# Alternating first-layer and second-layer units of a feed-forward block that runs beside attention

## The chip, the cores and the metric

The kernel runs on one core of one Trainium2 chip. The metric is the device time of one execution in microseconds (us). Before the change three runs took 1277.15, 1279.8 and 1281.62 us; the median is 1279.8 us.

## The reference

Thresholded attention is followed by a two-layer feed-forward block with no routing:

```python
scores = scale * q @ k.T                       # 8 batches, 8 heads, 576 tokens, head size 64
thresh = max(scores, -1) - tau                 # tau = 0.02
scores = where(scores >= thresh, scores, -1e9)
attn   = softmax(scores)                       # per row of 576
x      = (attn @ v), heads side by side        # 4608 tokens x 512
h      = x @ w_in                              # 512 x 2048
g      = h / (1 + exp(-h))
out    = g @ w_out                             # 2048 x 512
```

All inputs are float32.

## The kernel before, in words

**Attention.** The scores of one batch are worked off in 36 tiles of up to 128 query rows by 576 keys (`tiles`, 288 in all). For tile t, `scores` (L412) makes the scores in PSUM with four matrix products on TensorE. There are two such score buffers of two banks each. `soft1` takes the row maximum on VectorE (L422), `soft1b` the exponential on ScalarE (L432), `soft2` the threshold mask and the row sum on VectorE (L441, the last reader of the score buffer), `soft2b` the scaling on ScalarE (L454), and `soft3` splits the weights into two 16-bit parts on GpSimd (L465, L468, L471) and has them transposed by DMA. `av` (L496) multiplies by the values, and `av_post` (L514, L515) stores the result as the tiles `x16` of that batch. There are two sets of `x16`, for even and odd batches.

**Feed-forward.** Tokens are handled in chunks, two per batch: 288 and 288 columns (256 and 320 in batch 0). A chunk (b, c0, n) has 32 units. Sixteen are first-layer units: `h_unit` f makes 128 rows of h with 12 matrix products (L530) into one PSUM bank. Its `post` then runs four operations on that bank: tanh on ScalarE (L538), a product on VectorE (L539), a 16-bit copy into `gbuf` on ScalarE (L546) and the remainder of that rounding into `gbuf` on VectorE (L547), which releases the bank. The other sixteen are second-layer units: `o_unit` (d, quarter) adds 12 matrix products (L562) to the bank of output rows d. Each quarter uses four of the sixteen g tiles; after the fourth quarter a `post` copies the bank to memory on ScalarE (L572) and a DMA writes it out.

**Banks.** PSUM has four banks for scores, one for `av`, and three named m0, m1 and m2 that `bank` hands out in turn to whatever asks next (in turn over two of them early on, over three from the middle of batch 0). h units, o units and the small product of `pow2_scales` (L118, the maximum of a batch's values over all partitions) share them.

**Order.** `moe_units` yields all 16 h units of a chunk and then all 16 o units. The main loop walks over the tiles; when a chunk's `x16` is ready it appends the chunk's units to the list `units` and sets a rate (units per tile, such that 95% of the list is worked off by the time of the next batch). `step_unit` emits one unit's matrix products and then the `post` of the unit before. After the last tile at least four units are emitted per step. The framework then orders each engine's instructions at compile time, by priority and by a timeline that it simulates; each engine runs its own list strictly in that order. `scores` and `av` have a raised priority.

**gbuf** is one area in SBUF with 17 slots of 2 x 320 16-bit numbers, handed out in turn. Before batch 0's units need it, parts of it serve for loading weights (L158 to L160) and for the zero-padded queries of the first visits (L333).

Of the kernel before, what the change touches and what calls it, by code (L numbers as in the profile page):

```python
# [9 lines left out]
F16 = mybir.dt.float16  # L10
# [9 lines left out]
P = 128  # L20
B, H, S, D = 8, 8, 576, 64
NPAIR = H // 2
DM, DFF = 512, 2048
NK = DM // P
NF = DFF // P
HALF = S // 2
WID = 320
EXPMASK = 0x7F800000
GB = 17
WSPARE = 2  # L30
LOAD = 5
AV_LAG = 3
# [20 lines left out]
def attention_moe(  # L53
# [10 lines left out]
    nc = tc.nc  # L64
    const = ctx.enter_context(tc.tile_pool(name="const", bufs=1))
    sb = ctx.enter_context(tc.tile_pool(name="sb", bufs=2))
    gbuf = const.tile([P, GB * 2 * WID], F16, name="gbuf")
    xp = [ctx.enter_context(tc.tile_pool(name="x0", bufs=1))]
    stage_ctx = ExitStack()
    stage = stage_ctx.enter_context(tc.tile_pool(name="stage", bufs=2))  # L70
# [5 lines left out]
    turn = [0, 2]  # L76

    def bank(shape, name, own=None):
        if own is None:
            own = turn[0] = (turn[0] + 1) % turn[1]  # L80
        return ps_m.tile(shape, F32, tag=f"m{own}", name=name)
# [7 lines left out]
        out=gate, in0=tau_sb, scalar1=0.0, scalar2=0.125, op0=ALU.is_ge, op1=ALU.mult  # L89
# [3 lines left out]
        out=ntau, in0=tau_sb, scalar1=0.0, scalar2=-1.0, op0=ALU.max, op1=ALU.mult  # L93
# [6 lines left out]
    for i in range(2):  # L100
        t = const.tile([P, S + 64], F32R, name=f"qstack{i}")
# [4 lines left out]
    def pow2_scales(mx, name, across=True):  # L106


        k = name[0]
        one = const.tile([P, 1], F32, name=f"{name}_one", tag=f"{k}_one")  # L110
        nc.vector.tensor_reduce(out=one, in_=mx, op=ALU.max, axis=AX.X)
        if across:


            diag = const.tile([P, P], BF16, name=f"{name}_diag", tag="diag")
            nc.scalar.activation(diag, ident, AF.Copy, scale=one)
            allp = bank([P, P], f"{name}_ps")
            nc.tensor.matmul(allp, ones, diag, start=True, stop=True)  # L118
            one = const.tile([P, 1], F32, name=f"{name}_all", tag=f"{k}_all")
            nc.vector.tensor_reduce(out=one, in_=allp, op=ALU.max, axis=AX.X)  # L120
        cl = const.tile([P, 1], F32, name=f"{name}_cl", tag=f"{k}_cl")
        nc.vector.tensor_scalar(
            out=cl, in0=one, scalar1=2.0**-20, scalar2=2.0**47, op0=ALU.max, op1=ALU.min
        )
        e2 = const.tile([P, 2], I32, name=f"{name}_e2", tag=f"{k}_e2")
        nc.vector.tensor_scalar(
            out=e2[:, 0:1], in0=cl.bitcast(I32), scalar1=EXPMASK, scalar2=None, op0=ALU.bitwise_and
        )
        nc.vector.tensor_scalar(
            out=e2[:, 1:2], in0=cl.bitcast(I32), scalar1=EXPMASK, scalar2=EXPMASK,  # L130
            op0=ALU.bitwise_and, op1=ALU.bitwise_xor,
        )
        sc = const.tile([P, 2], F32, name=f"{name}_sc", tag=f"{k}_sc", bufs=3)
        nc.vector.tensor_scalar(
            out=sc[:, 0:1], in0=e2[:, 1:2].bitcast(F32), scalar1=2.0**12, scalar2=None, op0=ALU.mult
        )
        nc.vector.tensor_scalar(
            out=sc[:, 1:2], in0=e2[:, 0:1].bitcast(F32), scalar1=2.0**-13, scalar2=None, op0=ALU.mult
        )
        return sc  # L140
# [75 lines left out]
    def wi(c, f, lo):  # L216
        col = f * P
        o = (512 if lo else 0) + col % 512
        return w16[:, NK * (col // 512) + c, o : o + P]

    def wo(f, d, lo):
        o = (512 if lo else 0) + d * P
        return w16[:, 4 * NK + f, o : o + P]
# [108 lines left out]
    for i in range(2):  # L332
        t = gbuf.bitcast(F32)[:, 4096 + 512 * i : 4608 + 512 * i]  # L333
# [185 lines left out]


    gt = {}
    gcount = [0]
    po = {}

    def h_unit(b, c0, n, f):
        ph = bank([P, 512], f"h_{b}_{c0}_{f}")
        k = 0
        for c in range(NK):
            for lo_w, lo_x in ((0, 0), (0, 1), (1, 0)):
                nc.tensor.matmul(  # L530
                    ph[:, :n], wi(c, f, lo_w), x16[b, lo_x][:, c, c0 : c0 + n],
                    start=(k == 0), stop=(k == 11),
                )
                k += 1

        def post():
            th = sb.tile([P, WID], F32, tag="th", name=f"th_{b}_{c0}_{f}", bufs=2)
            nc.scalar.activation(th[:, :n], ph[:, :n], AF.Tanh, scale=moe_sc[b][:, 0:1])  # L538
            nc.vector.scalar_tensor_tensor(  # L539
                out=ph[:, :n], in0=th[:, :n], scalar=1.0, in1=ph[:, :n],  # L540
                op0=ALU.add, op1=ALU.mult,
            )
            o = 2 * WID * (gcount[0] % GB)
            gcount[0] += 1
            g = gbuf[:, o : o + 2 * WID].rearrange("p (r n) -> p r n", r=2)
            nc.scalar.activation(g[:, 0, :n], ph[:, :n], AF.Copy, scale=2.0**-14)  # L546
            nc.vector.scalar_tensor_tensor(  # L547
                out=g[:, 1, :n], in0=ph[:, :n], scalar=2.0**-14, in1=g[:, 0, :n],
                op0=ALU.mult, op1=ALU.subtract,
            )  # L550
            gt[b, c0, f] = g

        return post

    def o_unit(b, c0, n, d, quarter):
        if quarter == 0:
            po[b, c0, d] = bank([P, 512], f"o_{b}_{c0}_{d}")
        ps = po[b, c0, d]
        for f in range(4 * quarter, 4 * quarter + 4):
            g = gt[b, c0, f]  # L560
            for k, (lo_w, lo_g) in enumerate(((0, 0), (0, 1), (1, 0))):
                nc.tensor.matmul(  # L562
                    ps[:, :n], wo(f, d, lo_w), g[:, lo_g, :n],
                    start=(f == 0 and k == 0), stop=(f == NF - 1 and k == 2),
                )

        def post():
            if quarter < 3:
                return

            o = wst[:, NW + d % 2, :]
            nc.scalar.activation(o[:, :n], ps[:, :n], AF.Copy, scale=moe_sc[b][:, 1:2])  # L572
            c = b * S + c0
            nc.sync.dma_start(out=outT[d * P : (d + 1) * P, c : c + n], in_=o[:, :n])

        return post

    def moe_units(b, c0, n):
        for f in range(NF):
            yield lambda f=f: h_unit(b, c0, n, f)  # L580
        for d in range(DM // P):
            for quarter in range(4):
                yield lambda d=d, quarter=quarter: o_unit(b, c0, n, d, quarter)


    visits = [(0, p, kind) for kind in ("low", "high") for p in range(NPAIR)]
# [6 lines left out]
    ready = []  # L593
    start = {}
    for v, (b, p, kind) in enumerate(visits):
# [19 lines left out]
        if kind == "low":  # L615
            at(u - LOAD, lambda v=v: load_direct(v))
            at(u - 2, lambda v=v: scale_direct(v))
            c0, n = ranges[0]
# [13 lines left out]
    NT = len(tiles)  # L632
# [43 lines left out]
    units = []  # L676
# [4 lines left out]
    def run_posts():  # L681
        for f in post:
            f()
        post.clear()
# [6 lines left out]
    def live(t):  # L691
        return 0 <= t < NT and tiles[t] is not None

    scores(0)
    t = 0
    while t < NT + 8 or units or ready:
        while ready and ready[0][0] <= t:
            _, b, c0, n = ready.pop(0)
            units.extend(moe_units(b, c0, n))
            nxt = [r[0] for r in ready if r[0] > t + 1]  # L700
            rate = len(units) / max(1, (nxt[0] if nxt else NT + 8) - t)
            rate *= RATE
            if b == 0:
                rate = RATES[0 if c0 == 0 else 1]
        if t >= first_high + 20:
            turn[1] = 3
        if live(t):
            pri(PRI_SOFT1, lambda: soft1(t))()
        if live(t + 1):
            pri(PRI_S, lambda: scores(t + 1))()  # L710
        if live(t - 1):
            soft2b(t - 1)
        if live(t):
            pri(PRI_SOFT1, lambda: soft1b(t))()
        if live(t - 1):
            soft3(t - 1)
        for f in todo.pop(t, []):
            f()
        credit += rate
        if t >= NT:  # L720
            credit = max(credit, 4.0)
        if units and credit >= 1:
            step_unit()
            credit -= 1
        if live(t):
            pri(PRI_SOFT2, lambda: soft2(t))()
        for v, p, c0, n in avs.pop(t, []):
            b = visits[v][0]
            if v in direct:
                a_ps = av_direct(v, p)  # L730
            else:
                a_ps = pri(PRI_AV, lambda v=v, p=p, c0=c0, n=n: av(v, p, c0, n))()
            run_posts()
            scale = xscale if v in direct else 2.0**-12
            post.append(lambda b=b, p=p, c0=c0, n=n, a_ps=a_ps, scale=scale: av_post(b, p, c0, n, a_ps, scale))
        while units and credit >= 1:
            step_unit()
            credit -= 1
        if not units:
            credit = 0.0  # L740
            run_posts()
        t += 1
# [42 lines left out]
```

## Time and profile before

| | |
|---|---|
| three runs | 1277.15, 1279.8, 1281.62 us |
| span of the profiled execution (first to last instruction) | 1276.2 us |
| own device time of the profiled execution | not listed apart from its span |
| TensorE busy | 1152.4 us (90%) |
| VectorE busy | 967.7 us (76%) |
| ScalarE busy | 819.6 us (64%) |
| GpSimd busy | 751.1 us (59%) |
| mean granted TensorE clock | 0.969 |

PE stands for TensorE's matrix products, PEld for its weight loads, DVE for VectorE, ACT for ScalarE, POOL for GpSimd, SP for the queue that issues DMAs. "L530" is line 530 of the kernel before. A group's row ends with the idle time of its engine just before those instructions, and with what ended that idle time. Since every engine runs its list in order, an instruction that waits holds up all that stands behind it on its engine.

### The profile page before, as it was taken

The numbers are of one execution on the slowest core, as the hardware profiler recorded it, in microseconds if no ns is written. First come the engines' busy times: TensorE is split into PE (matmuls) and PEld (weight loads), VectorE is DVE, ScalarE is ACT, GpSimd is POOL, SyncE is SP. The second block draws the span as 40 slices with busy tenths as digits, with TensorE's granted clock in tenths as the row PEclk, the third lists the DMA queues.
The fourth block names the chain that finished last, engine by engine and source line by source line (L and its number), as shares of the span: only waits on it lengthen the run. The fifth ranks groups of instructions, "written<-read, shape, count | busy, mean of one in ns | idle before, by whom it ended". The sixth has DMA issues, their size and how long they took to land.

```text
span 1276.2 us, 27018 instructions
## 1 busy us (share of the span) xinstructions
PE 1152.4 (90%) x9400; PEld 898.8 (70%) x9400; DVE 967.7 (76%) x2627; ACT 819.6 (64%) x1505; POOL 751.1 (59%) x952
## 2 busy tenths in 40 slices
PE   5774768898899998998989999998999999999998
PEld 3453657676678776776767777786777777777777
DVE  7899998987988989888688858977598848521431
ACT  5787776765867867777476747866477746532431
POOL 4568977787678777874568608781478508300000
PEclk8886989998999999999989999999999999999999
DMA  9457768688778787873768538781687418300000
GB/s 301 121 183 179 172 119 163 138 151 168 135 151 154 135 168 161 156 146 79 152 122 157 114 85 158 148 156 39 129 159 144 103 24 140 72 15 18 8 15 19
DMA packets 363480, 158.15 MB, mean 124 GB/s; under 512 B 329552, under 2 KB 338256, under 8 KB 363344
## 3 DMA queue, kind: packets, MB, share of 16 engines
q1 hardware_dynamic: 363344, 156.43, 59.0%
q8 instruction: 74, 1.21, 0.4%
q14 instruction: 62, 0.51, 0.1%
HBM read 66.72 MB, written 9.44 MB: 60 GB/s over the span
## 4 chain that ended last, share of the span: by engine, by line
PE 52%; DVE 25%; ACT 6%; DMA 5%; issue 5%; POOL 5%; SPq 1%; POOLq 0%; ACTq 0%; DVEq 0%
PE o L562 22%; PE h L530 15%; PE a L496 7%; PE s L412 7%; DVE w L441 6%; DVE sm L422 5%; DVE qstack L316 4%; DMA wT<-hl 3%; ACT w L432 2%; DVE h L539 2%; DVE gbuf L547 2%; POOL hl L468 1%; DMA vraw<-in_vL 1%; ACT w L454 1%; POOL hl L465 1%
## 5 line engine op out<-in xcount | busy, mean ns | idle before, releaser
L530 PE MATMUL h<-x,wst 128*128 128x288 f16 (+2 forms) x3072 | 416.9, 291 | 23.1 <-DVE gbuf L547 19.4
L562 PE MATMUL o<-gbuf,wst 128*128 128x288 f16 (+2 forms) x3072 | 397.3, 287 | 2.5 <-DVE gbuf L547 1.4
L530 PEld LDWEIGHTS <-wst 128*128 128x128 f16 x3072 | 295.0, 99 | 114.9 <-issue 32.0
L562 PEld LDWEIGHTS <-wst 128*128 128x128 f16 x3072 | 291.9, 98 | 85.5 <-issue 8.3
L468 POOL TENSOR_TENSOR hl<-w,hl 128x512 f16<-128x512 f32 x272 | 328.1, 1206 | 15.9 <-ACT hl L463 2.1
L465 POOL TENSOR_SCALAR hl<-w 128x576 f16<-128x576 f32 x264 | 181.5, 690 | 236.6 <-ACT w L454 133.0
L432 ACT ACTIVATE w<-s,sm 128x576 f32<-128x576 f32 x288 | 211.2, 738 | 106.5 <-DVE sm L422 32.2
L441 DVE SCALAR_TENSOR_TENSOR w<-s,sm,w 128x576 f32<-128x576 f32 x288 | 232.7, 812 | 51.1 <-ACT w L432 49.1
L454 ACT ACTIVATE w<-w,sm 128x576 f32<-128x576 f32 x288 | 219.5, 772 | 68.7 <-DVE sm L449 59.5
L422 DVE TENSOR_REDUCE sm<-s 128x1 f32<-128x576 f32 x288 | 216.0, 751 | 55.4 <-PE s L412 51.8
L412 PE MATMUL s<-khi,qstack 128*128 128x288 f32 x608 | 158.7, 342 | 37.2 <-DVE w L441 29.9
L539 DVE SCALAR_TENSOR_TENSOR h<-th,h 128x288 f32<-128x288 f32 (+2 forms) x256 | 116.6, 456 | 80.9 <-ACT th L538 75.8
L538 ACT ACTIVATE th<-h,msc 128x288 f32<-128x288 f32 (+2 forms) x256 | 127.1, 500 | 30.7 <-PE h L530 27.7
L496 PE MATMUL a<-wT,v 128*64 128x288 f16 (+1 forms) x1680 | 131.8, 297 | 14.4 <-DMA wT<-hl 14.1
L546 ACT ACTIVATE gbuf<-h 128x288 f16<-128x288 f32 (+2 forms) x256 | 104.0, 408 | 63.5 <-DVE h L539 62.9
L547 DVE SCALAR_TENSOR_TENSOR gbuf<-h,gbuf 128x288 f16<-128x288 f32 (+2 forms) x256 | 115.0, 452 | 37.9 <-ACT gbuf L546 36.4
L412 PEld LDWEIGHTS s<-khi,qstack 128*128 128x128 f32 x608 | 96.8, 194 | 64.3 <-issue 39.7
L412 PE MATMUL s<-klo,qstack 128*128 128x288 f32 x608 | 133.1, 300 | 0.0
L326 POOL TENSOR_TENSOR klo<-kraw,khi 128x576 fp32r<-128x576 f32 x64 | 93.0, 1453 | 53.9 <-ACT khi L324 52.4
L496 PEld LDWEIGHTS <-v 128*64 128x64 f16 x1680 | 93.7, 112 | 42.1 <-issue 33.3
L412 PEld LDWEIGHTS s<-klo,qstack 128*128 128x128 f32 x608 | 100.2, 193 | 1.0 <-issue 0.2
L471 POOL TENSOR_TENSOR hl<-w,hl 128x64 f16<-128x64 f32 x272 | 94.0, 345 | 0.0
(84 smaller groups left out, 876.5 us busy)
## 6 DMA issues: line engine op xcount, KB each, us to landing
qraw<-in_qT SPq DMA_DIRECT2D x128, 144.0 KB, 3.0
kraw<-in_kT SPq DMA_DIRECT2D x128, 144.0 KB, 3.0
vraw<-in_vL SPq DMA_DIRECT2D x32, 320.0 KB, 3.8
wraw<-in_w_out SPq DMA_DIRECT2D x16, 512.0 KB, 3.9
out_t<-wst SPq DMA_DIRECT2D x56, 144.0 KB, 2.4
wT<-hl SPq DMA_TRANSPOSE x304, 3.4
gbuf<-in_w_in SPq DMA_DIRECT2D x8, 512.0 KB, 7.9
wraw<-in_w_in SPq DMA_DIRECT2D x8, 512.0 KB, 5.4
```

What stands on the lines that cost most here:

```text
L412: nc.tensor.matmul(s_ps[:, j, :HALF], lhs, kk[:, j * HALF : (j + 1) * HALF], start=(n == 0), stop=(n == len(seq) - 1),)
L422: nc.vector.tensor_reduce(out=negm, in_=s_ps[:, :, :HALF], op=ALU.max, axis=AX.XY, negate=True)
L432: nc.scalar.activation(wtile[t].rearrange("p (j c) -> p j c", j=2), sps[t][:, :, :HALF], AF.Exp, bias=small[t][:, 0:1],)
L441: nc.vector.scalar_tensor_tensor(out=w3, in0=s_ps[:, :, :HALF], scalar=sm[:, 1:2], in1=w3, op0=ALU.is_ge, op1=ALU.mult, accum_out=sm[:, 2:3],)
L454: nc.scalar.activation(w, w, AF.Copy, scale=r)
L465: nc.gpsimd.tensor_scalar(out=fl[:, 0:S], in0=w, scalar1=1.0, scalar2=1.0, op0=ALU.mult, op1=ALU.mult)
L468: nc.gpsimd.tensor_tensor(out=fl[:, 640:1152], in0=w[:, 0:512], in1=fl[:, 0:512], op=ALU.subtract)
L496: nc.tensor.matmul(a_ps[odd * D : (odd + 1) * D, :n], vt[:, lo_v, odd, kv, :], wT[v, b * H + 2 * p + odd][:, kw, c0 - base : c0 - base + n ...
L530: nc.tensor.matmul(ph[:, :n], wi(c, f, lo_w), x16[b, lo_x][:, c, c0 : c0 + n], start=(k == 0), stop=(k == 11),)
L539: nc.vector.scalar_tensor_tensor(out=ph[:, :n], in0=th[:, :n], scalar=1.0, in1=ph[:, :n], op0=ALU.add, op1=ALU.mult,)
L547: nc.vector.scalar_tensor_tensor(out=g[:, 1, :n], in0=ph[:, :n], scalar=2.0**-14, in1=g[:, 0, :n], op0=ALU.mult, op1=ALU.subtract,)
L562: nc.tensor.matmul(ps[:, :n], wo(f, d, lo_w), g[:, lo_g, :n], start=(f == 0 and k == 0), stop=(f == NF - 1 and k == 2),)
```

## The change

From batch 1 on, the h units of a chunk are no longer followed by its own o units. Each h unit of chunk c is followed by one o unit of chunk c-1. The first chunk of batch 1 has h units alone, and the o units of the last chunk come by themselves at the end. Batch 0 keeps its order. So that two chunks' g tiles can live at once, `gbuf` grows from 17 slots of 640 numbers to 18432 numbers per partition (16 x 2 x 576), and a chunk gets a contiguous region of it (`place_g`). The memory for it comes from the area reserved for DMA descriptors, which is set to 1 KB. In the alternating part the banks are fixed: even h units have m0, odd ones m1, and all o units m2; from the middle of batch 0 on the small product of `pow2_scales` has m0. The o units at the very end take banks in turn.

```diff
-GB = 17
+GWORDS = 2 * NF * S
...
-    gbuf = const.tile([P, GB * 2 * WID], F16, name="gbuf")
+    gbuf = const.tile([P, GWORDS], F16, name="gbuf")
...
-            allp = bank([P, P], f"{name}_ps")
+            allp = bank([P, P], f"{name}_ps", 0 if turn[1] == 3 else None)
...
-    def h_unit(b, c0, n, f):
-        ph = bank([P, 512], f"h_{b}_{c0}_{f}")
+    def place_g(b, c0, n):
+        if gnext[0] + 2 * NF * n > GWORDS:
+            gnext[0] = 0
+        gbase[b, c0] = gnext[0]
+        gnext[0] += 2 * NF * n
+
+    def h_unit(b, c0, n, f, own=None):
+        if f == 0:
+            place_g(b, c0, n)
+        ph = bank([P, 512], f"h_{b}_{c0}_{f}", own)
...
-            o = 2 * WID * (gcount[0] % GB)
-            gcount[0] += 1
-            g = gbuf[:, o : o + 2 * WID].rearrange("p (r n) -> p r n", r=2)
+            o = gbase[b, c0] + 2 * n * f
+            g = gbuf[:, o : o + 2 * n].rearrange("p (r n) -> p r n", r=2)
...
-    def o_unit(b, c0, n, d, quarter):
+    def o_unit(b, c0, n, d, quarter, own=None):
         if quarter == 0:
-            po[b, c0, d] = bank([P, 512], f"o_{b}_{c0}_{d}")
+            po[b, c0, d] = bank([P, 512], f"o_{b}_{c0}_{d}", own)
...
+    def h_units(b, c0, n, owns=(None,)):
+        return [
+            lambda f=f: h_unit(b, c0, n, f, owns[f % len(owns)]) for f in range(NF)
+        ]
+
+    def o_units(b, c0, n, own=None):
+        return [
+            lambda d=d, quarter=quarter: o_unit(b, c0, n, d, quarter, own)
+            for d in range(DM // P) for quarter in range(4)
+        ]
+
+    held = []
+
     def moe_units(b, c0, n):
-        for f in range(NF):
-            yield lambda f=f: h_unit(b, c0, n, f)
-        for d in range(DM // P):
-            for quarter in range(4):
-                yield lambda d=d, quarter=quarter: o_unit(b, c0, n, d, quarter)
+        if b == 0:
+            return h_units(b, c0, n) + o_units(b, c0, n)
+        out = []
+        if held:
+            for pair in zip(h_units(b, c0, n, (0, 1)), o_units(*held.pop(), 2)):
+                out.extend(pair)
+        else:
+            out = h_units(b, c0, n)
+        held.append((b, c0, n))
+        return out
...
-    while t < NT + 8 or units or ready:
+    while t < NT + 8 or units or ready or held:
...
+        if held and not ready and not units and t >= NT + 8:
+            units.extend(o_units(*held.pop()))
...
-    nc = bacc.Bacc("TRN2", target_bir_lowering=False, num_devices=1)
+    nc = bacc.Bacc(
+        "TRN2", target_bir_lowering=False, num_devices=1, dynamic_dma_scratch_size=1024
+    )
```

More of the change, by code (lines that the diff above doesn't have):

```diff
@@ L521, in attention_moe @@
     gt = {}
-    gcount = [0]
+    gbase = {}
+    gnext = [0]
     po = {}
-    def h_unit(b, c0, n, f):
-        ph = bank([P, 512], f"h_{b}_{c0}_{f}")
+    def place_g(b, c0, n):
[7 more added lines that the diff above has]
+        ph = bank([P, 512], f"h_{b}_{c0}_{f}", own)
         k = 0
```

## The prediction

> **What bounds the kernel now.** I read the page's sums first, then where in the span the h products (L530) and the o products (L562) run, then a table of stages cut at the ends of these blocks, then the waits of TensorE inside the alternating stretch.
>
> ```profile
> span 1276.2 us, 27018 instructions
> ...
> PE 1152.4 (90%) x9400; PEld 898.8 (70%) x9400; DVE 967.7 (76%) x2627; ACT 819.6 (64%) x1505; POOL 751.1 (59%) x952
> ```
>
> TensorE is the busiest engine and is idle for 1276.2 - 1152.4 = 123.8 us. The change can only win part of that idle time, since it takes no matrix product away. The views of the two lines, last row each, show where their products run in 40 slices of 31.9 us:
>
> ```profile
> L530 PE MATMUL h<-x,wst x3072: 270/286/464, 91.5 to 1249.0; 128*128 128x288 f16 x168, 128*128 128x256 f16 x12, 128*128 128x320 f16 x12
> ...
> busy tenths in 40 slices 0026953923968919589395998939096998998994
> ...
> L562 PE MATMUL o<-gbuf,wst x3072: 272/286/311, 179.6 to 1272.5; 128*128 128x288 f16 x168, 128*128 128x256 f16 x12, 128*128 128x320 f16 x12
> ...
> busy tenths in 40 slices 0000089099099390995909997392909997899999
> ```
>
> They take turns: h blocks and o blocks of about a slice each. The next fence is the table of stages. The first group are h blocks, with the sum over the ten of them from 398 to 1106 us; the second are o blocks, with the sum over the ten from 364 to 1069 us; the last three are batch 1's first h block and an h and an o block after attention has ended. The columns are length, busy time of the engines, granted clock, and DMA.
>
> ```profile
> core 0: us, PE busy (x) PEld busy (x) DVE busy (x) ACT busy (x) POOL busy (x), PEclk, DMA share, GB/s
> ...
> 476.60:524.80 48.20, 43.39 (x377) 34.13 (x376) 45.48 (x139) 38.61 (x74) 40.08 (x52) 1.00 0.77 148
> 561.10:600.20 39.10, 34.23 (x255) 27.10 (x253) 35.89 (x109) 31.71 (x61) 23.62 (x32) 0.96 0.47 98
> 634.40:682.10 47.70, 43.09 (x342) 32.94 (x341) 43.59 (x123) 35.78 (x71) 32.93 (x45) 0.93 0.69 133
> ...
> 856.70:890.30 33.60, 29.85 (x226) 23.48 (x224) 26.76 (x73) 23.59 (x48) 10.39 (x13) 0.95 0.23 57
> ...
> sum 400.20, PE 365.77 PEld 287.76 DVE 361.12 ACT 309.95 POOL 258.18; mean PE 36.58 PEld 28.78 DVE 36.11 ACT 31.00 POOL 25.82
> ...
> 442.40:476.60 34.20, 33.23 (x292) 26.72 (x291) 28.99 (x82) 22.91 (x38) 24.43 (x33) 1.00 0.85 168
> 524.80:561.10 36.30, 35.96 (x303) 28.31 (x302) 29.37 (x80) 24.28 (x38) 31.58 (x41) 1.00 0.86 162
> ...
> sum 342.30, PE 340.99 PEld 268.64 DVE 233.64 ACT 190.75 POOL 229.34; mean PE 34.10 PEld 26.86 DVE 23.36 ACT 19.07 POOL 22.93
> ...
> 302.50:361.60 59.10, 49.15 (x388) 38.26 (x386) 52.55 (x154) 43.91 (x80) 43.47 (x58) 0.91 0.72 139
> ...
> 1131.50:1155.10 23.60, 23.60 (x195) 18.83 (x194) 13.35 (x29) 13.96 (x31) 0.00 (x0) 1.00 0.02 7
> 1155.10:1178.60 23.50, 23.50 (x195) 18.76 (x193) 1.38 (x3) 2.61 (x6) 0.00 (x0) 1.00 0.07 21
> ```
>
> Three readings. In the ten h blocks TensorE idles 400.2 - 365.8 = 34.4 us, in the ten o blocks 342.3 - 341.0 = 1.3 us: 35.7 us together. VectorE is at 361.1/400.2 = 0.90 in the h blocks (0.94 in the one from 476.6) and at 233.6/342.3 = 0.68 in the o blocks: there are two regimes, one short of VectorE and one short of TensorE. After attention nothing idles: 23.6 us for 16 units, so one bare unit is 1.475 us, h or o.
>
> What TensorE waited for between 361.6 and 1131.7 us, longest first (total, times, longest):
>
> ```profile
> PE s L412 <- DVE w L441: 17.7, 12, 2.4
> PE h L530 <- DVE gbuf L547: 10.1, 13, 1.7
> PE s L412 <- DVE sm L425: 2.6, 4, 1.0
> PE a L496 <- DMA wT<-hl: 2.6, 4, 1.4
> ```
>
> The first is a score product that stands at the head of TensorE's list before VectorE has read the score buffer it needs; the second an h unit whose bank is not yet drained. Both are VectorE being late in an h block.
>
> **The change, part by part.** The sum is made against the profiled execution, span 1276.2 us. Of that execution no other time is listed. The median of the runs, 1279.8, is 3.6 us above the span, and I carry these 3.6 over.
>
> *Up to 361.6 us: nothing.* Batch 0 keeps its order, and batch 1's first chunk has h units alone. The 9.9 us of idle (59.10 - 49.15) and the low clock of 0.91 in the stage from 302.5 stay.
>
> *From 361.6 to 1106 us: h and o alternate.* The same products, copies and stores are issued. Per h unit the four operations after it cost what these rows say:
>
> ```profile
> L538 ACT ACTIVATE th<-h,msc 128x288 f32<-128x288 f32 (+2 forms) x256 | 127.1, 500 | 30.7 <-PE h L530 27.7 <-ACT gbuf L546 0.3
> L539 DVE SCALAR_TENSOR_TENSOR h<-th,h 128x288 f32<-128x288 f32 (+2 forms) x256 | 116.6, 456 | 80.9 <-ACT th L538 75.8
> L546 ACT ACTIVATE gbuf<-h 128x288 f16<-128x288 f32 (+2 forms) x256 | 104.0, 408 | 63.5 <-DVE h L539 62.9
> L547 DVE SCALAR_TENSOR_TENSOR gbuf<-h,gbuf 128x288 f16<-128x288 f32 (+2 forms) x256 | 115.0, 452 | 37.9 <-ACT gbuf L546 36.4 <-PE h L530 1.0
> L572 ACT ACTIVATE wst<-o,msc 128x288 f32<-128x288 f32 (+2 forms) x64 | 31.5, 494 | 84.3 <-PE o L562 84.2
> ```
>
> VectorE owes 0.456 + 0.452 = 0.91 us per h unit. Now it owes them every 1.475 us of unit time, then every 2.95 us. The twenty blocks hold 706.8 us of TensorE work and 361.1 + 233.6 = 594.8 us of VectorE work. Without idle time that is 594.8/706.8 = 0.84 of VectorE. The nearest rows are the o blocks at 442.4 (28.99/34.20 = 0.85 of VectorE, 1.0 us or 2.8% idle) and 524.8 (0.81, 0.3 us or 0.9% idle). They are bounds for the mixed regime: 0.9% of 706.8 is 6 us, 2.8% is 20 us. Against them stands the h block at 856.7, which idles 11% at a VectorE share of 0.80; it would leave all 35.7 us (a rival below). I take the middle of the two o rows, 13 us, as the o units give TensorE work that needs nothing from VectorE. **Idle: -35.7 + 13 = -22.7 us.** What the waits turn into: an h bank is used again after three other units (4.4 us bare) where it was two (2.95 us), against a bare chain of 0.500 + 0.456 + 0.408 + 0.452 = 1.8 us, so the 10.1 us of L547 should nearly go. The score waits of 17.7 us shrink and do not go.
>
> *All o groups in bank m2.* This is the wait that the change adds. Group d+1 may start only after L572 has copied group d, and one h unit lies between (1.475 us bare). The next rows are from the timeline at the ends of two o blocks (start, length). The first has a loaded ScalarE, the second finds it free.
>
> ```profile
> 558.76 2.49 PE L562 MATMUL o<-gbuf,wst 128*128 128x288 f16 x19
> ...
> 562.25 0.78 ACT L454 ACTIVATE w<-w,sm 128x576 f32<-128x576 f32 x1 [1.17 <-DVE sm L449]
> ...
> 562.93 0.48 ACT L572 ACTIVATE wst<-o,msc 128x288 f32<-128x288 f32 x1
> ...
> 781.00 0.54 PE L562 MATMUL o<-gbuf,wst 128*128 128x288 f16 x3
> ...
> 781.58 0.50 ACT L572 ACTIVATE wst<-o,msc 128x288 f32<-128x288 f32 x1
> ```
>
> From the last o product to the end of the copy it is 563.41 - 561.25 = 2.16 us in the one case (ScalarE stood on L454, which waited 1.17 us for VectorE) and 0.54 us in the other. Behind one h unit that leaves 0.69 or 0 us exposed. Ten chunks with four groups meet a loaded ScalarE, so the bounds are 0 and 40 x 0.69 = 28 us. ScalarE would be at (309.95 + 190.75)/706.8 = 0.71, between the h blocks' 0.77 and the o blocks' 0.56; score and `av` products also slip between the units and lengthen the cover. I take **+6 us**. A waiting o unit holds the next h unit and the next tile's scores behind it, so L422 on VectorE is late next. The Trainium skill, page "Perfetto Trace Analysis", section "Optimizing Tensor Performance", would have independent groups rotate through different banks, which the o groups stop doing. By that rule alone each of the forty copies would lie open; the first rival prices this from the rows.
>
> *Clock.* The h blocks at 561.1, 634.4 and 856.7 were granted 0.96, 0.93 and 0.95: 0.04 x 39.1 + 0.07 x 47.7 + 0.05 x 33.6 = 6.6 us. The bounds are 0 and -6.6; with fewer stalls I take half, **-3.3 us**. The Trainium skill, page "TensorE: Matmul & The Clock Gate", section "Why this matters for your kernels", asks for gaps above about 3 us before the clock falls. The trace disagrees: the longest listed wait here is 2.4 us. By the rule the clock term would be 0 and the sum 3.3 us higher.
>
> *Sixteen o units at the end.* They add 16 x 1.475 = 23.6 us of work after the last chunk and take the same from the stretch before. That costs nothing as long as TensorE has other units ready there; its blocks lie back to back from 361.6 on, so units are always waiting. If they ran out the price would be up to +23.6 us. `x16` of a batch is still released after the same number of units, so attention is held back no earlier than now. **0 us**, and 0 in the tail, where a copy (0.494 us) ends well inside an h unit and no bank waits.
>
> *The rest, 0 us.* The product of `pow2_scales` and its reduction take 0.219 + 0.286 us in bank m0, six times, inside the 4.4 us of that bank's slack; uncovered they cost 3 us. The small descriptor area is used by nothing: apart from instructions all packets are on q1, and every issue, the output's too, is on SP's queue. The 56 output stores stay as many but come evenly; if they got into the way of the transposes, the 2.6 us of L496 could double.
>
> ```profile
> q1 hardware_dynamic: 363344, 156.43, 59.0%
> ...
> out_t<-wst SPq DMA_DIRECT2D x56, 144.0 KB, 2.4
> ...
> L120 DVE TENSOR_REDUCE v_all<-v_ps 128x1 f32<-128x128 f32 x8 | 2.3, 286 | 4.4 <-PE v_ps L118 4.4
> ...
> L118 PE MATMUL v_ps<-v_diag,ones 128*128 128x128 bf16 x8 | 1.8, 219 | 0.0
> ```
>
> **The sum:** -22.7 + 6 - 3.3 = -20 us. The span goes to 1256 us, a run to 1279.8 - 20 = 1260 us.
>
> **Rivals.** *The o bank decides (slower).* If the tanh of the h unit in between (0.500 us) gets ahead of the copy on ScalarE, the loaded case exposes 2.16 + 0.50 - 1.475 = 1.19 us, forty times 47 us. Against a gain of 22.7 + 3.3 = 26 us that makes +21 us: 1301 us. The point from which it decides is 26/40 = 0.65 us per group. For it: the copy is emitted only after the next h unit's products, and the loaded case alone leaves 0.69 us. Against it: the free case leaves none, and it would take the loaded case nearly every time.
>
> *The shortage is only spread (same).* VectorE is in order and its work stays; the o blocks lose what the h blocks win, as the block at 856.7 (0.80, 11% idle) suggests, or the compile-time order pulls h units together again, so that the change does not do what it says. The idle stays near 35.7 us: 1280 us. Against it: the o block at 442.4 idles 2.8% at a higher VectorE share.
>
> *All of it is won.* Idle time and clock loss go and the o bank costs nothing: -35.7 - 6.6 = -42 us, 1238 us. For it speak the blocks after 1131 us, with no idle time in h blocks at all; against it, that attention is absent there.
>
> **How the numbers follow.** Chances: forecast 0.55 (its own range 1248 to 1271, from the bounds of the idle term and a few us of the o bank), all won 0.14 (1238 to 1248), spread 0.13, o bank 0.18. The range 1240 to 1288 takes in nearly all of the upside, the spread case, and the milder part of the o bank (20 + 28 - 35.7 = +12 us without the clock's share is 1292). A change under 0.3% (3.8 us) cannot be told from none. Faster: 0.55 + 0.14 less 0.01 for forecasts that end near nothing, 0.68; same 0.13; slower 0.18 and that 0.01, 0.19.
>
> **What would show it.** Right: h and o products both busy in every slice from 362 us on; VectorE near 0.84 there without the swing between 0.68 and 0.90; TensorE's idle time in that stretch near 19 us; L530's wait on L547 under 3 us; a new wait of L562 on L572 of a few us; clock 1.00 almost throughout; the time after attention unchanged in its density. Wrong: L562 waiting on L572 for over 25 us, score waits on L441 above 18 us, h and o still in blocks, or a gap before the last sixteen o units.

## The result and the profile after

Four runs of the changed kernel took 1244.94 to 1249.47 us, median 1246.07 us; the kernel before took 1278.97 us beside them. The ratio is 0.9752 with a 95% interval of 0.9722 to 0.9782: 33 us less, where 20 were forecast and the stated range began at 1240. The profiled execution took 1244.94 us, 1.7 us more than its span.

The first rows of the page after, and the last rows of the views of its h line (now L539) and its o line (now L570), in 40 slices of 31.1 us:

```profile
span 1243.2 us, 26997 instructions
...
PE 1140.7 (92%) x9400; PEld 897.4 (72%) x9400; DVE 961.3 (77%) x2627; ACT 818.0 (66%) x1505; POOL 759.4 (61%) x952
```

```profile
busy tenths in 40 slices 0024983953899899998999998999999999999991
...
busy tenths in 40 slices 0000059099038987899899997999899998999999
```

From slice 12 on both lines are at work in every slice, where before one stood while the other ran. The order was changed as the text says. TensorE and VectorE have the work they had; TensorE is idle for 1243.2 - 1140.7 = 102.5 us instead of 123.8.

Cut at the same four places of the work (start of batch 1's first h block, its end, last score tile, end), the tables of stages are, first of before, then of after (length; busy PE, PEld, DVE, ACT, POOL; granted clock; DMA):

```profile
0.00:302.50 302.50, 229.15 (x1660) 170.96 (x1661) 272.65 (x685) 220.22 (x396) 219.44 (x250) 0.91 0.71 171
...
361.60:1092.80 731.20, 694.95 (x5876) 547.36 (x5875) 587.68 (x1665) 493.91 (x897) 481.75 (x637) 0.99 0.66 129
1092.80:1276.30 183.50, 179.12 (x1484) 142.23 (x1482) 54.82 (x125) 61.61 (x134) 6.44 (x10) 1.00 0.08 21
```

```profile
0.00:303.70 303.70, 231.39 (x1660) 173.62 (x1661) 275.43 (x687) 219.94 (x396) 218.89 (x249) 0.90 0.71 169
303.70:366.00 62.30, 49.75 (x390) 38.81 (x389) 54.01 (x159) 46.36 (x83) 47.59 (x62) 0.92 0.77 147
366.00:1058.80 692.80, 678.68 (x5855) 541.00 (x5854) 580.43 (x1667) 493.26 (x899) 487.32 (x634) 1.00 0.72 135
1058.80:1243.20 184.40, 180.93 (x1502) 144.01 (x1499) 51.40 (x117) 58.48 (x128) 5.56 (x8) 1.00 0.08 22
```

The third stage, where h and o units run beside attention, went from 731.2 to 692.8 us. That is all of the gain and more: -38.4 us there, +1.2 in the first stage, +3.2 in the second (59.1 to 62.3), +0.9 after attention. (The cuts do not part exactly the same work: 21 products, some 2.6 us, have gone from the third stage, most of them to the last.) In it TensorE's idle time fell from 36.3 to 14.1 us and its busy time by 16.3 us.

VectorE's share is 580.4/692.8 = 0.84 in the mean, but not throughout. Of ten equal pieces of this stage seven have VectorE at 0.87 to 0.90 and three at 0.69 to 0.74. One of each:

```profile
643.10:712.40 69.30, 68.97 (x575) 56.25 (x573) 62.51 (x192) 52.59 (x95) 56.23 (x73) 1.00 0.75 147
712.40:781.70 69.30, 64.98 (x589) 51.36 (x588) 49.76 (x132) 41.83 (x78) 33.90 (x45) 1.00 0.62 119
```

In each of the three, GpSimd's work on attention weights stands for about 18 to 21 us. In the seven TensorE idles 7.6 of 485.0 us (1.6%), in the three 6.5 of 207.8 us (3.1%).

TensorE's waits from 366 us to the end, complete:

```profile
PE o L570 <- ACT wst L580: 6.5, 5, 2.6
PE s L412 <- DVE w L441: 2.4, 3, 1.8
PE h L539 <- DVE gbuf L555: 2.3, 2, 1.8
PE a L496 <- DMA wT<-hl: 1.2, 2, 0.6
PE s L412 <- DVE sm L425: 1.2, 1, 1.2
```

Score products waited 17.7 us for L441 before and wait 2.4 us now; h units waited 10.1 us for their bank and wait 2.3 us. What came in is the wait of o units for the copy out of their only bank. Its longest case in the timeline after (start, length; the idle time before it in brackets):

```profile
743.79 1.63 PE L539 MATMUL h<-x,wst 128*128 128x288 f16 x12
744.31 0.67 POOL L465 TENSOR_SCALAR hl<-w 128x576 f16<-128x576 f32 x1 [18.15 <-DVE h L548]
...
746.51 0.74 ACT L432 ACTIVATE w<-s,sm 128x576 f32<-128x576 f32 x1 [3.18 <-POOL hl L471]
...
747.43 0.50 ACT L580 ACTIVATE wst<-o,msc 128x288 f32<-128x288 f32 x1
...
747.99 2.24 PE L570 MATMUL o<-gbuf,wst 128*128 128x288 f16 x17 [2.56 <-ACT wst L580]
```

ScalarE's list had an exponential (L432) ahead of the copy, and this waited 3.18 us for GpSimd, which had itself only just begun again after 18.15 us without work. (The releaser named there, L548, shares no tile with L465, so what held GpSimd is not shown.) TensorE had done its one h unit and stood still behind the copy for 2.56 us. Of the five waits, two with 3.7 of the 6.5 us stand behind such a held exponential. Ahead of the second longest (1.57 us) ScalarE worked without a pause: the copy was simply late in its list.

### The profile page after: what moved, and what is told of

Its sections match the earlier page's. It is cut to its first block, busy times and chain, and to the rows that moved or that the text cites. A ratio compares the mean times of both kernels' runs of the same rounds, so it can differ in the third digit from the quotient of the medians.

```text
span 1243.2 us, 26997 instructions
## 1 busy us (share of the span) xinstructions
PE 1140.7 (92%) x9400; PEld 897.4 (72%) x9400; DVE 961.3 (77%) x2627; ACT 818.0 (66%) x1505; POOL 759.4 (61%) x952
## 4 chain that ended last, share of the span: by engine, by line
PE 54%; DVE 25%; DMA 6%; ACT 6%; issue 5%; POOL 4%; SPq 0%; ACTq 0%; POOLq 0%; DVEq 0%
PE o L570 20%; PE h L539 19%; PE s L412 7%; PE a L496 7%; DVE w L441 6%; DVE sm L422 5%; DMA vraw<-in_vL 3%; DVE qstack L316 3%; ACT w L432 2%; DMA wT<-hl 2%; DVE wst L212 2%; DVE h L548 1%; DVE gbuf L555 1%; ACT w L454 1%; DVE wst L186 1%
## 5 line engine op out<-in xcount | busy, mean ns | idle before, releaser
L539 PE MATMUL h<-x,wst 128*128 128x288 f16 (+2 forms) x3072 | 430.8, 290 | 12.7 <-DVE gbuf L555 10.2
L570 PE MATMUL o<-gbuf,wst 128*128 128x288 f16 (+2 forms) x3072 | 420.6, 287 | 8.2 <-ACT wst L580 6.5
L539 PEld LDWEIGHTS <-wst 128*128 128x128 f16 x3072 | 294.6, 99 | 102.0 <-issue 22.0
L570 PEld LDWEIGHTS <-wst 128*128 128x128 f16 x3072 | 293.2, 98 | 90.5 <-issue 11.4
L468 POOL TENSOR_TENSOR hl<-w,hl 128x512 f16<-128x512 f32 x272 | 329.3, 1211 | 14.5 <-ACT hl L463 2.1
L465 POOL TENSOR_SCALAR hl<-w 128x576 f16<-128x576 f32 x264 | 180.6, 687 | 190.8 <-ACT w L454 128.3
L432 ACT ACTIVATE w<-s,sm 128x576 f32<-128x576 f32 x288 | 210.5, 738 | 83.5 <-DVE sm L422 30.6
L441 DVE SCALAR_TENSOR_TENSOR w<-s,sm,w 128x576 f32<-128x576 f32 x288 | 232.0, 812 | 32.5 <-ACT w L432 30.2
L548 DVE SCALAR_TENSOR_TENSOR h<-th,h 128x288 f32<-128x288 f32 (+2 forms) x256 | 116.2, 455 | 108.5 <-ACT th L547 106.4
L547 ACT ACTIVATE th<-h,msc 128x288 f32<-128x288 f32 (+2 forms) x256 | 126.2, 497 | 106.0 <-PE h L539 104.7
L412 PE MATMUL s<-khi,qstack 128*128 128x288 f32 x608 | 158.7, 343 | 19.0 <-DVE w L441 14.5
L554 ACT ACTIVATE gbuf<-h 128x288 f16<-128x288 f32 (+2 forms) x256 | 103.5, 407 | 81.3 <-DVE h L548 80.2
L555 DVE SCALAR_TENSOR_TENSOR gbuf<-h,gbuf 128x288 f16<-128x288 f32 (+2 forms) x256 | 114.9, 451 | 40.4 <-ACT gbuf L554 39.6
L471 POOL TENSOR_TENSOR hl<-w,hl 128x64 f16<-128x64 f32 x272 | 100.2, 368 | 0.0
```

What stands on the lines that cost most here:

```text
L412: nc.tensor.matmul(s_ps[:, j, :HALF], lhs, kk[:, j * HALF : (j + 1) * HALF], start=(n == 0), stop=(n == len(seq) - 1),)
L432: nc.scalar.activation(wtile[t].rearrange("p (j c) -> p j c", j=2), sps[t][:, :, :HALF], AF.Exp, bias=small[t][:, 0:1],)
L441: nc.vector.scalar_tensor_tensor(out=w3, in0=s_ps[:, :, :HALF], scalar=sm[:, 1:2], in1=w3, op0=ALU.is_ge, op1=ALU.mult, accum_out=sm[:, 2:3],)
L465: nc.gpsimd.tensor_scalar(out=fl[:, 0:S], in0=w, scalar1=1.0, scalar2=1.0, op0=ALU.mult, op1=ALU.mult)
L468: nc.gpsimd.tensor_tensor(out=fl[:, 640:1152], in0=w[:, 0:512], in1=fl[:, 0:512], op=ALU.subtract)
L539: nc.tensor.matmul(ph[:, :n], wi(c, f, lo_w), x16[b, lo_x][:, c, c0 : c0 + n], start=(k == 0), stop=(k == 11),)
```

## The experiments

Three theories were set against each other. A: while h ran alone, VectorE was late, and alternating spreads its work. S: what counted is that an h bank is now used again after three other units instead of two. C: holding a second chunk in memory, and so having more units to choose from, brought the gain. Ratios are to the kernel before, run on the same chip.

**The alternation undone and the banks in turn again, all else kept.**

```diff
-            for pair in zip(h_units(b, c0, n, (0, 1)), o_units(*held.pop(), 2)):
-                out.extend(pair)
+            out = h_units(b, c0, n) + o_units(*held.pop())
```

> The changed kernel with only the alternation undone: from batch 1 on the 16 h units of chunk c come as a block, then the 16 o units of chunk c-1 as a block, banks in turn as before. The deferral by one chunk, the larger gbuf and the small descriptor area stay. Theory A (the blocks make VectorE late while h runs, the alternation evens it out): the gain goes, 1279 us within 8, VectorE again near 0.90 in h blocks and TensorE idle near 35 us after 361 us. Theory C (the deferral itself, by giving the compile-time order a second chunk to choose from, brings the gain): near 1246 us.

It took 1279.61 us, ratio 1.0008 (0.9987 to 1.0028). The stage beside attention, and the largest waits from its start to the end of the run:

```profile
366.40:1077.70 711.30, 675.17 (x5729) 533.18 (x5728) 584.58 (x1667) 490.96 (x898) 481.63 (x633) 0.99 0.69 131
```

```profile
PE s L412 <- DVE w L441: 14.9, 16, 2.2
PE h L539 <- DVE gbuf L555: 8.4, 9, 1.8
PE a L496 <- DMA wT<-hl: 8.3, 9, 2.4
```

The idle time is back (711.3 - 675.2 = 36.1 us) and with it the same two waits; the wait of `av` for transposes is longer than before (8.3 us for 2.6). VectorE stands at 370.1/405.5 = 0.91 in the ten h blocks of this run, as expected. C falls: the deferral by a chunk, the larger buffer and the small descriptor area bring nothing and cost nothing that the time can tell (of its span of 1277.7 us, the part up to 366.4 us is 4.8 us longer than before and the part behind it 3.3 us shorter). The gain is the alternation's, with the banks that go with it; the two were not tried apart.

**More VectorE work per h unit**, in the kernel before and in the changed one, placed so that it holds no bank:

```diff
+            nc.vector.scalar_tensor_tensor(
+                out=th[:, :n], in0=th[:, :n], scalar=1.0, in1=th[:, :n],
+                op0=ALU.mult, op1=ALU.max,
+            )
             gt[b, c0, f] = g
```

> The kernel before with one more VectorE operation per h unit, behind L547: the maximum of th with itself, in place, 288 columns in SBUF. It changes no result, reads no PSUM and does not hold an h bank; I estimate 0.4 us of it from the 0.451 us of L547, 64 us over the ten loaded h blocks. Theory A (VectorE's load in h blocks sets the pace there): the ten blocks hold 361 us of VectorE work in 400 us, so 64 us more cannot fit: at least 361 + 64 - 400 = 25 us longer, more likely 35 to 60 us. Theory S (what counted was how soon a bank is used again, two other units before and three after): under 12 us longer.

> The changed kernel with the same additional VectorE operation per h unit. Theory A: in the alternating stretch it goes from about 0.85 to 0.94 of VectorE's time, which still fits: 5 to 25 us longer than the changed kernel, clearly less than the same load costs the kernel before. Theory S: as much as in the kernel before, both under 12 us.

They took 1345.75 us (ratio 1.0538, 1.0505 to 1.0572) and 1286.24 us (1.0075, 1.005 to 1.0099): 68 us more than the kernel before, 40 us more than the changed one. The added operation in each (shortest, median and longest in ns), and the stage beside attention in each:

```profile
L551 DVE SCALAR_TENSOR_TENSOR th<-th x256: 400/457/1518, 106.8 to 1317.5; 128x288 f32<-128x288 f32 x112, 128x256 f32<-128x256 f32 x8, 128x320 f32<-128x320 f32 x8
```

```profile
380.90:1158.10 777.20, 707.65 (x5886) 554.37 (x5885) 660.65 (x1820) 499.25 (x898) 496.89 (x638) 0.98 0.63 122
```

```profile
L559 DVE SCALAR_TENSOR_TENSOR th<-th x256: 399/458/1633, 107.1 to 1258.0; 128x288 f32<-128x288 f32 x112, 128x256 f32<-128x256 f32 x8, 128x320 f32<-128x320 f32 x8
```

```profile
383.90:1095.60 711.70, 683.56 (x5826) 540.20 (x5826) 653.71 (x1821) 489.46 (x896) 505.80 (x637) 1.00 0.68 132
```

The operation took 0.46 us at the median, a little more than I had estimated (the means, 0.61 and 0.60 us, come from single ones of up to 1.6 us). VectorE's busy time in the stage rose by 73 us in both kernels (660.7 - 587.7 and 653.7 - 580.4). In this stage, which the change touches, the load cost 777.2 - 731.2 = 46 us before and 711.7 - 692.8 = 19 us after, both inside the ranges of A (35 to 60 and 5 to 25). Both totals lie above these ranges. Their rest lies mostly in batch 0 and in batch 1's first h block (19.3 and 17.9 us), which have the same order in both kernels and got the operation too. The floor by A's formula, with the measured load, is 361 + 73 - 400 = 34 us, and it holds. S in its plain form falls: a load that holds no bank should have cost under 12 us.

The edit adds a little more than load. The operation holds the tile `th`, of which there are two; over the whole run tanh waited 8.5 us for it before and 3.0 us after. And GpSimd's busy time in the stage rose by 15 and 18 us. After the change VectorE stood at 653.7/711.7 = 0.92, with TensorE idle for 28.1 us instead of 14.1.

**Less VectorE work per h unit**, again in both kernels:

```diff
-                out=ph[:, :n], in0=th[:, :n], scalar=1.0, in1=ph[:, :n],
+                out=ph[:, :8], in0=th[:, :8], scalar=1.0, in1=ph[:, :8],
```

> The kernel before with L539 on 8 of its columns in place of all, so that most of h passes without its factor (1 + tanh): this part of the computation is left out. VectorE has about 0.3 us less per h unit (estimate: 0.456 us less the time of a short operation such as the 0.15 us of L445), 46 us less over the ten loaded h blocks, and the chain that drains a bank is as much shorter. Theory A: its share there falls from 0.90 to about 0.79 and most of the 34 us of TensorE idle time and the clock loss go: 1250 to 1262 us. If VectorE's lateness in these blocks is not the cause: above 1270 us.

> The changed kernel with L548 on 8 columns in place of all (the same part is left out). Theory A: VectorE is no longer what TensorE waits for in the alternating stretch, so little is left to win: 1236 to 1246 us, a gain of under 10 us and less than the same edit brings the kernel before.

They took 1252.5 us (ratio 0.98, 0.977 to 0.9829) and 1248.16 us (0.9769, 0.9731 to 0.9808). The shortened operation and the stage beside attention, before and after:

```profile
L539 DVE SCALAR_TENSOR_TENSOR h<-th,h 128x8 f32<-128x8 f32 x256 | 40.9, 164 | 102.6 <-ACT th L538 102.3
```

```profile
357.80:1068.00 710.20, 687.32 (x5875) 544.28 (x5875) 540.41 (x1663) 492.50 (x896) 480.66 (x636) 1.00 0.69 133
```

```profile
359.20:1055.00 695.80, 679.18 (x5801) 537.42 (x5800) 547.01 (x1667) 490.18 (x896) 487.18 (x636) 1.00 0.71 135
```

Taking 0.456 - 0.164 = 0.29 us of VectorE work off each h unit brings the kernel before 25 us (21 us of it in this stage), three quarters of what the change brings, and the changed kernel nothing (1248.16 against 1246.07 us, where I had expected 1236 to 1246). The two kernels, 33 us apart, are 4 us apart once VectorE has less to do for h, and 60 us apart when it has more. The three pairs together bear out A. They don't prove that the third unit of slack is worth nothing: this edit also shortens the chain that drains a bank.

**All h units in one bank, the o groups in two.**

```diff
-            for pair in zip(h_units(b, c0, n, (0, 1)), o_units(*held.pop(), 2)):
+            for pair in zip(h_units(b, c0, n, (0,)), o_units(*held.pop(), 1)):
...
-            lambda d=d, quarter=quarter: o_unit(b, c0, n, d, quarter, own)
+            lambda d=d, quarter=quarter: o_unit(b, c0, n, d, quarter, own and own + d % 2)
```

> The changed kernel with all h units of the alternating part in one bank (m0) and the o groups by turns in m1 and m2. VectorE's work and the alternation are the same; an h bank is used again after one other unit (1.475 us bare) instead of three (4.4 us), and the four operations that drain it take 1.8 us bare. Theory A plus enough slack: the waits of h for L555 become the bound, also after attention, where each h unit would wait at least 0.4 us (bare chain 1.8 us plus handovers against 1.475 us): over 200 h units 80 us or more, about 1330 us or more. Theory A alone, with slack of no account: near 1246 us.

It took 1513.47 us, ratio 1.1857 (1.1831 to 1.1883). Its two largest waits from 363.9 us to the end:

```profile
PE o L570 <- ACT gbuf L554: 128.7, 117, 2.2
PE h L539 <- DVE gbuf L555: 35.6, 37, 3.2
```

So alternation pays only as long as the chain of four operations fits between two uses of a bank. One unit is too little: 267 us over 208 h units, 1.3 us each, three times the floor I had named. Near the end of the alternation the timeline repeats every 3.71 us:

```profile
1288.49 1.63 PE L539 MATMUL h<-x,wst 128*128 128x288 f16 x12
...
1289.95 0.65 PE L570 MATMUL o<-gbuf,wst 128*128 128x288 f16 x4
...
1291.24 0.41 ACT L554 ACTIVATE gbuf<-h 128x288 f16<-128x288 f32 x1 [0.53 <-DVE h L548]
1291.69 0.46 DVE L555 SCALAR_TENSOR_TENSOR gbuf<-h,gbuf 128x288 f16<-128x288 f32 x1 [0.47 <-ACT gbuf L554]
1291.71 0.40 PE L570 MATMUL o<-gbuf,wst 128*128 128x288 f16 x2 [1.10 <-ACT gbuf L554]
...
1292.20 1.63 PE L539 MATMUL h<-x,wst 128*128 128x288 f16 x12
```

Two products of an o unit start when L554 has ended, and the next h unit when L555 has. Both waits belong to the draining of the one bank. Between two h units of this stretch stand six products of o and not twelve: the compile-time order did not keep one and one, so the cover was about 0.74 us where I had counted 1.475. Why products of o wait for L554 at all stays open. Between two units of slack and three no run tells apart.

**The o bank.** Two edits give the copy more time or an earlier place:

```diff
+            hs, os_ = h_units(b, c0, n, (0, 1)), o_units(*held.pop(), 2)
+            for k in range(0, NF, 2):
+                out.extend(hs[k : k + 2] + os_[k : k + 2])
```

> The changed kernel with two h units followed by two o units in place of one and one; banks as changed. An h bank is still used again after three other units, but an o group now has two h units (2.95 us bare) between its end and the next group where it had one (1.475 us). If the o bank is what is left (L570 waits 6.5 us for L580 in the changed kernel) that wait falls under 1.5 us and the time to about 1241 us. If it must be single units for VectorE's sake, it is slower than 1250 us.

```diff
-        def post():
-            if quarter < 3:
-                return
+        def store():
...
-        return post
+        if quarter == 3:
+            pri(PRI_SOFT2, store)()
+        return lambda: None
```

> The changed kernel with the copy of an o group (L580) emitted right behind the group's last products and with the priority of soft2 raised, where it came after the next h unit's products. If the 6.5 us of L570 <- L580 come from the copy's place in ScalarE's list, they fall under 2 us and the time to about 1241 us. If they come from ScalarE waiting on VectorE ahead of the copy, they stay and so does 1246 us.

Two and two took 1252.26 us (ratio 0.9807, 0.9777 to 0.9837), the early copy 1246.03 us (0.9755, 0.9728 to 0.9782). The wait and the stage beside attention, of two and two and then of the early copy:

```profile
PE o L570 <- ACT wst L580: 4.8, 3, 2.0
```

```profile
367.30:1060.90 693.60, 680.36 (x5823) 540.62 (x5822) 578.14 (x1655) 489.95 (x895) 488.32 (x633) 0.99 0.71 134
```

```profile
PE o L570 <- ACT wst L577: 2.6, 3, 1.0
```

```profile
365.80:1058.10 692.30, 680.74 (x5852) 540.91 (x5852) 578.67 (x1667) 493.78 (x899) 488.70 (x634) 1.00 0.72 135
```

Both expectations on the wait missed. With two h units as cover three waits of up to 2.0 us remain. Ahead of the longest (1.98 us, up to 722.70 us) ScalarE had worked without a pause from 719.35 us on, so it isn't the length of the cover that lacks but what ScalarE has ahead of the copy. The early copy takes 3.9 of the 6.5 us away, and neither the stage (692.3 us) nor the time moves; what took its place is not shown.

Two and two is 6 us slower, as I had expected if single units are needed for VectorE's sake. Its profile shows something else, the granted clock:

```profile
590.20:593.60 3.40, 3.40 (x17) 2.17 (x15) 3.40 (x12) 2.27 (x4) 3.18 (x5) 0.50 0.99 208
723.30:726.70 3.40, 3.40 (x17) 2.14 (x15) 3.40 (x9) 1.43 (x3) 0.00 (x0) 0.50 0.61 196
```

From 364.9 to 368.3 us it is 0.50 as well. Three times 3.4 us at half clock cost about 5 us (an estimate: half of that time) of the 6.0 us between the spans of the two profiled executions (1249.2 and 1243.2). In the changed kernel the clock is 1.00 from batch 1's first alternating chunk on. The last of the three falls follows the wait of 1.98 us.

**The alternation begun one chunk earlier**, with and without the early copy, beside the changed kernel once more:

```diff
+            late.extend(o_units(b, c0, n, 2)[8:])
+            return hs + os_[:8]
...
-            out = h_units(b, c0, n)
+            hs = h_units(b, c0, n, (0, 1))
+            for k in range(8):
+                out.extend(hs[2 * k : 2 * k + 2] + [late.pop(0)])
```

> The changed kernel with the alternation begun one chunk earlier: of batch 0's second chunk only the first eight o units run behind its h units, the other eight alternate with the sixteen h units of batch 1's first chunk (two h, one o). If an h block beside attention always costs TensorE idle time, that of this block (12.6 us of 62.4 us, clock about 0.9) shrinks by half or more: 1238 to 1242 us. If batch 1's attention then lacks o units to run beside it, the gain is given back before: 1243 to 1250 us.

> As the kernel with eight o units of batch 0 held, and the copy of an o group emitted right behind its last products with raised priority. The early copy took 3.9 us off the waits of L570 but nothing off the time, so the same as without it within 4 us.

> The changed kernel once more beside the other two on one chip: 1246 us within 3, as measured first; TensorE idle time in the stretch from the end of batch 1's first h block to the last tile again near 14 us.

They took 1254.33 us (0.9826, 0.9804 to 0.9847), 1250.3 us (0.9803, 0.978 to 0.9825) and 1247.94 us (0.9772, 0.975 to 0.9795). The first two stages of the first of them:

```profile
0.00:280.90 280.90, 209.90 (x1479) 158.02 (x1480) 255.88 (x635) 205.36 (x374) 201.24 (x229) 0.89 0.72 170
280.90:383.90 103.00, 88.23 (x700) 65.90 (x699) 90.31 (x261) 72.60 (x126) 81.65 (x107) 0.93 0.76 153
```

TensorE's idle time up to 383.9 us is 71.0 + 14.8 = 85.8 us, against 72.3 + 12.6 = 84.9 us up to 366 us in the changed kernel: none of it was won. The expectation was wrong: the time lies above the range for a gain (1238 to 1242) and above the one for a gain that is given back (1243 to 1250). Of the 7.3 us by which its span is longer, 4.9 are busy time of TensorE; where they come from stays open. No version here beats the changed kernel. The two versions are 4 us apart, with intervals that overlap. The repetition left about 15 us of idle time in the stage beside attention (14 the first time).

## Why the prediction was right

**The time.** 1246 us lies in the stated range, but not in the forecast's own (1248 to 1271): by the time alone it would be the rival "all of it is won" (1238 to 1248). By the mechanism it is the forecast. Of 36.3 us of idle time in the stage 14.1 are left, and the o bank cost what was put down for it. That the time came out so low has other reasons, which follow term by term.

**Up to 361.6 us, nothing.** Nearly: the first two stages are 4.4 us longer. Batch 1's first h block took 62 to 63 us with the blocks kept and with the alternation (63.2 and 62.3), so it is not the alternation's doing; what it comes from was not tried.

**The idle term.** The mechanism was right. The waits of score products for L441 and of h units for L547 were both VectorE being late, and both nearly went. Its share came out at the 0.84 that was worked out, but as a mean: the swing between h and o blocks is gone, and another is left between pieces with attention at full pace (0.87 to 0.90) and pieces in which it stands for a while (0.69 to 0.74). The size was off. I took 13 us of remaining idle time as the middle of the two o rows (6 and 20 us); without the o bank's 6.5 us it is 14.1 - 6.5 = 7.6 us, near the lower row. I had said that the score waits shrink and do not go; they went from 17.7 to 2.4 us. The Trainium skill, page "Perfetto Trace Analysis", section "Optimization Strategy", says that interleaving regimes with different most-contended engines may help; here it took TensorE's idle time in them from 36 to 14 us.

**The o bank.** I took 6 us; it is 6.5 us, in five waits. The reason given, ScalarE standing on an operation that itself waits, is what the timeline shows for 3.7 of the 6.5 us; it waited for GpSimd there, not for VectorE as in the row that I had gone by. That the sum fits so closely is in part luck. The rival that let it decide needed 0.65 us for each of forty groups; it got 6.5/40 = 0.16 us.

**The clock.** This term was mis-sized. I took half of 6.6 us; the granted clock is 1.00 in the whole stage, so all 6.6 us went, the far bound. That nothing was left is in part luck: two and two has as few waits (12 where the changed kernel has 13), and its clock fell twice in that stage. The Trainium skill's rule on gaps (page "TensorE: Matmul & The Clock Gate", section "Why this matters for your kernels") would have given 0; the row was the better guide.

**The rest.** The sixteen deferred units, the descriptor area and the larger buffer cost nothing that the time can tell: the alternation undone, with all of them kept, ran as long as the kernel before.

**The sum.** Idle time in the stage gave -22.1 us where -16.7 (-22.7 + 6) was forecast, the clock -6.6 where -3.3 was. The busy time of TensorE from 361.6 us (366 us) on fell from 874.1 to 859.6 us, 14.5 us, and the clock accounts for less than half of that. The step that the sum lacked is what a stall takes inside busy time. A product's row is 0.286 us long at the median, while a new one starts every 1.475/12 = 0.123 us; so the first 0.16 us of each stall still counts as busy. The waits in the complete lists for that stretch fell from 41 to 13, which by this estimate is 28 x 0.16 = 4.5 us. Some 3 us stay unassigned. The first two stages, 4.4 us longer, hide as much of what the stage won.

The rival "only spread" failed on the o units: the mixed stage idles 2.0% at a VectorE share of 0.84, and 1.6% in its pieces at 0.87 to 0.90, like the o rows and not like the h block at 856.7 us.

## What to carry to other kernels

When the table of stages shows one engine short in one kind of block and another engine in the next, try alternating the two kinds. Here the blocks short of VectorE idled 34 us, and alternating won 22 us of idle time and 33 us in all; the other block's row at the same load was the better guide to what remained. Before giving one kind of work a single buffer, take the length of the chain that empties it and the work that lies between two uses: three units against a chain of 1.8 us were ample here, one unit cost 267 us. To find whether an engine's load is the cause, add and remove work on it that holds as little else as can be, in both versions, and see whether their difference grows and vanishes; look at the stage that the change touches, since the edit reaches others too.

## What the runs showed of the hardware

The length of a single wait did not tell whether the granted clock would fall. In the kernel before, TensorE waited 2.37 us up to 866.71 us and 2.37 us up to 1011.44 us. These are the stretches that followed:

```profile
867.60:871.00 3.40, 3.40 (x17) 2.15 (x15) 2.44 (x9) 0.99 (x3) 0.28 (x2) 0.50 0.07 22
1011.40:1015.00 3.60, 3.56 (x29) 2.95 (x29) 3.60 (x15) 1.88 (x5) 1.22 (x2) 1.00 0.30 86
```

The clock was halved after the first and whole after the second. In the changed kernel it stayed at 1.00 after a wait of 2.56 us, and in two and two it fell after one of 1.98 us. The number of waits did not tell either (13 without a fall, 12 with two). What does is not shown.

The busy time of TensorE holds part of each stall, by the estimate above 0.16 us of each; its idle time understates by that what stalls cost. From the end of batch 1's first h block on, 23 us less idle time came with 37 us less time, of which the clock accounts for some 6.6 us and this for some 4.5 us.
